# GpSimd keeps only the maxima across partitions in the first group; its clamps, memsets and low halves of weights go to VectorE and ScalarE

## The chip, the core and the metric

The kernel runs on one core of a Trainium2 chip. The core has five engines that run their own instruction queues and meet at semaphores: TensorE (PE, with its weight loads as PEld), VectorE (DVE), ScalarE (ACT), GpSimd (POOL) and SyncE (SP, which here issues every DMA). The metric is the device time of one execution in microseconds (us), lower is better; a comparison quotes the median of several executions.

## The reference: what is computed

Attention inside chunks of 64 positions, and then a two-layer network on its output:

```python
scores = scale * np.matmul(q_c, k_c.transpose(0, 1, 2, 4, 3))   # 8 batches, 8 heads, 9 chunks of 64x64
attn = np.exp(scores - max); attn = attn / (sum + 1e-09)
x = (attn @ v_c) put as (4608 tokens, 512)
h = x @ w_in            # 512 -> 2048
g = h - np.tanh(h)
out = g @ w_out         # 2048 -> 512
```

All of it is in float32.

## The kernel before, in words

**Tiling.** Tokens are taken 128 at a time (a "pair" of chunks): 36 pairs, in nine groups of four (512 tokens). For each group the network runs over 16 columns of 128 in the hidden layer (fc = 0 to 15): `gemm1` makes `ph` from x and w_in, `shrink` makes g from `ph`, and `gemm2` adds g times w_out into the four output tiles `po`. To reach float32 accuracy each operand is cut into a high and a low half (x: `xh`, `xl`; w_in: `wih`, `wil`; g: `gh`, `gl`; w_out: `woh`, `wol`), and three matmuls are made instead of one.

**Scales.** The 16-bit halves need a power of two as scale. For two fc of w_in at a time (index j = 0 to 7), for the values v of four pairs, and in the later groups for q, k and v, ScalarE sums absolute values per partition (`spread`, tiles named `junk`, result in `sums`). `power` then clamps the sums from below with TINY (POOL, tile `wall` or `xall`), takes the maximum across partitions (POOL, `partition_all_reduce`, tile `wtop` or `xtop`), and on DVE keeps the exponent bits (`from_w`, `earlyfrom`) and inverts (`to_w`, `earlyto`). `wih` and `wil` wait for `to_w`; `xh` and `xl` wait for `earlyto`.

**The first group** also has everything that is done once: the 16 MB of weights arrive as 64-bit patterns (`raw_in`, `raw_out`), `merged` turns them into float32 with one ACT and three DVE instructions per fc, and `weights` cuts the halves. `wol` (w_out minus its high half) is made on DVE for fc 0 and 1 and on POOL for the other 14. The attention of the first eight pairs (class `Early`) runs between this work. It keeps q and v in block-diagonal tiles (`qbd`, `vbd`, four buffers each) whose empty corners are zeroed once; buffers 0 and 1 are zeroed on DVE and ACT, buffers 2 and 3 on POOL. `identity` for the PE transposes is also made on POOL.

**Order.** PLAN is a list of tokens. Up to its bar, SP and PE keep the order of the tokens as written, and a scheduler orders the other engines; behind the bar the scheduler orders all of them, with its own idea of how long things take. At run time each engine takes its own queue strictly in order. The tokens that the prediction uses: `S` scores of a pair, `T` its transpose (PE, line 161, tile `psa`<-`ident`,`s`), `V` its values (PE, line 261), `N`/`n` its softmax division (on DVE, or head by head on ACT, line 244), `F` filler matmuls, `c` the cutting of a weight, `g` gemm1 with `shrink`, `h` gemm2. PE does the last tokens before its first network matmul in this order: T1, V0, V1, F7, S3, T2, g0.0.

**The later groups** (1 to 8) run the network on finished weights; attention of the next group (class `Late`) runs beside it, with its q, k and v scales made by the same `power`.

Of the kernel before, what the change touches and what calls it, by code (L numbers as in the profile page):

```python
# [11 lines left out]
F32 = mybir.dt.float32  # L12
# [3 lines left out]
U32 = mybir.dt.uint32  # L16
AF = mybir.ActivationFunctionType
ALU = mybir.AluOpType
# [3 lines left out]
P = 128  # L22
# [17 lines left out]
TINY = 2.0 ** -100  # L40
EXPONENT = 0x7F800000
# [13 lines left out]
def attn_ffn_kernel(ctx: ExitStack, tc: tile.TileContext, qE, kE, vE, qL, kL, vL, w_in, w_out, out):  # L55
# [7 lines left out]
    nc = tc.nc  # L63
# [11 lines left out]
    wo = [[None, None] for _ in range(FC)]  # L75
# [16 lines left out]
    def spread(pool, a, out):  # L92

        shape = [a.shape[0], *a.shape[1:]]
        junk = pool.tile(shape, BF16, name=f"junk{math.prod(shape[1:])}", bufs=1)
        nc.scalar.activation(junk, a, AF.Abs, scale=2.0 ** -12, accum_out=out)

    def power(pool, name, sums, to, back):


        n = sums.shape[1]
        al = pool.tile([P, n], F32, name=f"{name}all", bufs=2)
        nc.gpsimd.tensor_scalar_max(al, sums, TINY)
        top = pool.tile([P, n], F32, name=f"{name}top", bufs=2)
        nc.gpsimd.partition_all_reduce(top, al, channels=P, reduce_op=bass_isa.ReduceOp.max)
        if back.shape[1] < n:
            nc.vector.reduce_max(out=back, in_=top, axis=AX.X)
            top = back
        nc.vector.tensor_single_scalar(back.bitcast(U32), top.bitcast(U32), EXPONENT, op=ALU.bitwise_and)
        nc.vector.reciprocal(out=to, in_=back)  # L110


# [12 lines left out]
    def merged(w, raw):  # L125
        low, up = raw[:, :, 0], raw[:, :, 1]
        nc.scalar.activation(w.bitcast(F32), up.bitcast(F32), AF.Abs, scale=2.0 ** -112)
        nc.vector.tensor_single_scalar(w, w, 3, op=ALU.logical_shift_left)  # L128
        nc.vector.scalar_tensor_tensor(out=w, in0=low, scalar=29, in1=w, op0=ALU.logical_shift_right, op1=ALU.bitwise_or)  # L129
        nc.vector.scalar_tensor_tensor(out=w, in0=up, scalar=0x80000000, in1=w, op0=ALU.bitwise_and, op1=ALU.bitwise_or)  # L130

    def weights(pool, fc, part):
        if part:
            w = pool.tile([P, DM], U32, name="w_out", bufs=2)
            merged(w, raw_out.pop(fc))
            w = w.bitcast(F32)
            nc.scalar.copy(out=wo[fc][0], in_=w)
            (nc.vector if fc < 2 else nc.gpsimd).tensor_sub(wo[fc][1], w, wo[fc][0])  # L138
            return
        j, i = divmod(fc, 2)  # L140
        if i == 0:
            w_in_f[j] = pool.tile([P, 2, DM], U32, name="w_in", bufs=2), pool.tile([P, 2], F32, name="wsum", bufs=2)
        w, sums = w_in_f[j]
        merged(w[:, i], raw_in[j][:, i])
        w = w.bitcast(F32)
        spread(pool, w[:, i], sums[:, i:i + 1])
        if i == 0:
            return
        to = to_w[:, j:j + 1]
        power(pool, "w", sums, to, from_w[:, j:j + 1])  # L150
        h, l = wi[j]
        for i in range(2):
            nc.scalar.activation(h[:, i], w[:, i], AF.Copy, scale=to)  # L153
            nc.vector.scalar_tensor_tensor(out=l[:, i], in0=w[:, i], scalar=to, in1=h[:, i], op0=ALU.mult, op1=ALU.subtract)  # L154
# [9 lines left out]
    class Early:  # L164
# [3 lines left out]
        def __init__(self, pool, psum, bufs, zeros):  # L168
            self.pool, self.psum, self.st, self.bufs = pool, psum, defaultdict(dict), bufs
            self.qbd, self.vbd = (  # L170
                [pool.tile([P, 4, P, 2], F32, name=f"{n}{i}", bufs=1) for i in range(bufs)] for n in ("qbd", "vbd")
            )
            for i in range(bufs):
                for t in self.qbd[i], self.vbd[i]:
                    for r, o in ((slice(0, D), slice(D, P)), (slice(D, P), slice(0, D))):
                        if i > 1:
                            nc.gpsimd.memset(t[r, :, o], 0.0)
                        elif t is self.qbd[i]:
                            nc.vector.memset(t[r, :, o], 0.0)
                        else:  # L180
                            nc.scalar.copy(out=t[r, :, o], in_=zeros[r].rearrange("p (hp d two) -> p hp d two", hp=4, two=2))
# [16 lines left out]
        def powers(self, ps_):  # L198

            sums = self.pool.tile([P, len(ps_)], F32, name=f"vsum{len(ps_)}", bufs=1)  # L200
            for j, p in enumerate(ps_):
                spread(self.pool, self.st[p]["v"].rearrange("p hp d two -> p (hp d two)"), sums[:, j:j + 1])
            to, back = (const.tile([P, 1], F32, name=f"early{n}{ps_[0]}") for n in ("to", "from"))
            power(self.pool, "x", sums, to, back)
            for p in ps_:
                self.st[p]["to"] = to
            return back
# [63 lines left out]
    class Late:  # L271
# [16 lines left out]
        def sums(self, g, n):  # L288

            d = self.st[f"g{g}"]  # L290
            if n == "q":
                d["sums"] = self.pool.tile([P, 3], F32, name="sums", bufs=2)
            some = self.raw[n][:, :SIZES[g]]
            spread(self.pool, some, d["sums"][:, "qkv".index(n):"qkv".index(n) + 1])
            if n != "v":
                return
            d["to"], d["from"] = (self.pool.tile([P, 3], F32, name=m, bufs=2) for m in ("to", "from"))
            power(self.pool, "x", d["sums"], d["to"], d["from"])
            d["exp"] = self.pool.tile([P, 1], F32, name="exp", bufs=2)
            nc.vector.scalar_tensor_tensor(out=d["exp"], in0=d["from"][:, 0:1], scalar=scale, in1=d["from"][:, 1:2], op0=ALU.mult, op1=ALU.mult)  # L300
            from_x[g] = d["from"][:, 2:3]
# [171 lines left out]
    pool = first.enter_context(tc.tile_pool(name="first", bufs=2))  # L473
# [2 lines left out]
    nc.vector.memset(warm, 0.0)  # L476
    ident = pool.tile([P, P], F32, name="ident", bufs=1)
    make_identity(nc, ident)
    att = Early(pool, [psum, ps_a], 4, warm)


# [3 lines left out]
    def step(token):  # L485
# [17 lines left out]
        elif kind in "ME":  # L503
            att.largest(n)
            att.exponents(n, summed=kind == "E")
        elif kind in "Nn":
            att.sums(n)
            att.normalise(n, by_head=kind == "n")
        elif kind == "T":
            att.transpose(n)  # L510
            att.weights(n)
        elif kind == "V":
            att.values(n)
            att.result(n, *((x, n) if n < SIZES[0] else (nx, n - SIZES[0])))
        elif kind == "c":
            for k in (0, 1) if part is None else (part,):
                weights(raw, n, k)
        elif kind == "g":
            ff.gemm1(n, *((0, 4) if part is None else (2 * part, 2 * part + 2)))
            ff.shrink()  # L520
        elif kind == "h":
            ff.gemm2()
        elif kind == "Y":
            first_psum.close()
            att.psum = [ps_a]
            ps_o2 = ctx.enter_context(tc.tile_pool(name="ps_o2", bufs=1, space=PSUM, reuse_waits="tile"))
            ff.room(ps_o2, range(2, 4))
            pools.append(ps_o2)
        elif kind == "Z":
            first.close()  # L530
            late = ctx.enter_context(tc.tile_pool(name="late_weights", bufs=1, reuse_waits="tile"))
            weight_tiles(late, range(EARLY_FC, FC))
# [62 lines left out]
```

## Time and profile before

| | us |
|---|---|
| median of 3 runs (lowest, highest) | 915.82 (914.55, 917.6) |
| the profiled execution's own time | 919.06 |
| its span, first to last instruction | 917.2 |
| PE busy | 871.7 (95%) |
| DVE busy | 533.2 (58%) |
| ACT busy | 469.5 (51%) |
| POOL busy | 43.6 (5%) |

The profiled execution took 1.86 us more than its span, and 3.24 us more than the median of the three runs. PE is busy 95% of the span as an average; the slices of the span show where the other 5% lies. Idle time of an engine is put down in the profile to the instruction that ended it, or to "issue", where the engine waited for nothing that the profile shows.

### The profile page before, as it was taken

How to read it: one execution, taken by the hardware profiler on the slowest of the kernel's cores; microseconds unless marked ns; L12 is line 12 of the kernel's file. 1: busy time of each engine (PE TensorE's matmuls, PEld its weight loads, DVE VectorE, ACT ScalarE, POOL GpSimd, SP SyncE). 2: the span in 40 equal slices, each digit the busy share in tenths (PEclk: the TensorE clock that was granted, in tenths of full speed). 3: DMA queues.
4: the chain of work that ended last, by engine and by line, in shares of the span. 5: the costliest groups of instructions: out<-in, count | busy, mean ns of one | idle time of the engine just before them, and what ended most of it. 6: DMA issues, size and time to landing. Idle time of an engine off the chain costs nothing.

```text
span 917.2 us, 13175 instructions
## 1 busy us (share of the span) xinstructions
PE 871.7 (95%) x5163; PEld 571.1 (62%) x5163; DVE 533.2 (58%) x940; ACT 469.5 (51%) x820; POOL 43.6 (5%) x70
## 2 busy tenths in 40 slices
PE   7379897799999999999999999999999999999997
PEld 5367763456665666566656665666566666665665
DVE  4758686539776557555755575557555755533222
ACT  6548765357664646464646464646464644333221
POOL 2002121320000000000000000000000000000000
PEclk7779899999999999999999999999999999999999
DMA  8682232034222212220222122212221011001001
GB/s 230 211 243 74 93 118 88 1 138 103 67 72 81 58 24 74 77 58 24 72 78 58 25 73 77 58 24 73 77 58 25 12 47 24 13 12 46 1 1 46
DMA packets 61373, 62.71 MB, mean 68 GB/s; under 512 B 32640, under 2 KB 40832, under 8 KB 61312
## 3 DMA queue, kind: packets, MB, share of 16 engines
q1 hardware_dynamic: 61312, 61.88, 23.4%
q8 instruction: 40, 0.66, 0.3%
q14 instruction: 21, 0.17, 0.1%
HBM read 45.09 MB, written 9.44 MB: 59 GB/s over the span
## 4 chain that ended last, share of the span: by engine, by line
PE 84%; DVE 5%; issue 5%; ACT 4%; POOL 1%; DMA 1%; SPq 0%; ACTq 0%; POOLq 0%; DVEq 0%
PE po L437 40%; PE ph L416 38%; PE psa L362 2%; PE psa L328 2%; PE psa L261 1%; PE psa L213 1%; ACT s L231 1%; DVE w_in L129 1%; POOL wol L138 1%; DVE w_in L130 1%; ACT wih L153 1%; DVE w_in L128 1%; DVE w_out L129 0%; DVE w_out L130 0%; DVE t L425 0%
## 5 line engine op out<-in xcount | busy, mean ns | idle before, releaser
L437 PE MATMUL po<-woh,gh 128*128 128x512 f32 x576 | 245.7, 428 | 2.8 <-ACT gh L428 2.8
L437 PE MATMUL po<-wol,gh 128*128 128x512 f32 x576 | 227.0, 395 | 2.3 <-POOL wol L138 2.3
L437 PE MATMUL po<-woh,gl 128*128 128x512 f32 x576 | 225.8, 395 | 1.3 <-DVE gl L429 1.3
L425 DVE SCALAR_TENSOR_TENSOR t<-ph,sig,t 128x512 f32<-128x512 f32 (+1 forms) x148 | 108.7, 734 | 168.2 <-ACT t L424 168.2
L416 PEld LDWEIGHTS <-wih 128*128 128x128 f16 x1184 | 106.8, 99 | 156.8 <-issue 41.5
L424 ACT ACTIVATE t<-ph,sig 128x512 f32<-128x512 f32 (+1 forms) x148 | 99.9, 675 | 165.4 <-PE ph L416 165.1
L416 PE MATMUL ph<-xh,wih 128*128 128x512 f16 (+1 forms) x592 | 150.3, 377 | 24.2 <-ACT xh L268 16.5
L429 DVE TENSOR_TENSOR gl<-t,gh 128x512 fp32r<-128x512 f32 (+1 forms) x148 | 101.5, 686 | 114.3 <-ACT gh L428 114.1
L428 ACT CAST gh<-t 128x512 fp32r<-128x512 f32 (+1 forms) x148 | 89.5, 604 | 133.5 <-PE po L437 93.2
L416 PE MATMUL ph<-xl,wih 128*128 128x512 f16 (+1 forms) x592 | 149.3, 375 | 0.0
L416 PE MATMUL ph<-xh,wil 128*128 128x512 f16 (+1 forms) x592 | 149.1, 374 | 0.0
L437 PEld LDWEIGHTS po<-woh,gh 128*128 128x128 f32 x576 | 109.0, 189 | 33.7 <-ACT gh L428 4.4
L437 PEld LDWEIGHTS po<-wol,gh 128*128 128x128 f32 x576 | 108.8, 189 | 25.0 <-POOL wol L138 3.6
L437 PEld LDWEIGHTS po<-woh,gl 128*128 128x128 f32 x576 | 108.1, 188 | 25.9 <-DVE gl L429 2.6
L416 PEld LDWEIGHTS <-wil 128*128 128x128 f16 x592 | 57.9, 98 | 66.8 <-DVE wil L154 1.3
L320 DVE SCALAR_TENSOR_TENSOR v16l<-rawv,to,v16h 64x512 f16<-64x512 f32 x56 | 41.7, 745 | 3.8 <-ACT v16h L319 2.9
L311 DVE SCALAR_TENSOR_TENSOR q16l<-rawq,to,q16h 64x512 f16<-64x512 f32 x56 | 41.6, 743 | 2.2 <-ACT q16h L310 1.4
L319 ACT ACTIVATE v16h<-rawv,to 64x512 f16<-64x512 f32 x56 | 40.1, 716 | 4.9 <-PE psa L362 3.4
L310 ACT ACTIVATE q16h<-rawq,to 64x512 f16<-64x512 f32 x56 | 40.2, 718 | 3.1 <-DVE exp L300 1.2
L336 ACT ACTIVATE s<-s,exp 128x512 f32<-128x512 f32 x28 | 20.1, 720 | 30.1 <-DVE s L335 30.1
L348 ACT CAST a<-s 128x512 f16<-128x512 f32 x28 | 17.2, 615 | 21.6 <-DVE s L342 19.5
L460 DVE COPY t<-po 128x512 f32<-128x512 f32 x18 | 12.4, 691 | 26.7 <-PE po L437 14.3
(98 smaller groups left out, 779.8 us busy)
## 6 DMA issues: line engine op xcount, KB each, us to landing
out<-t SPq DMA_DIRECT2D x36, 256.0 KB, 2.1
raw_in<-w_in SPq DMA_DIRECT2D x16, 512.0 KB, 5.3
raw_out<-w_out SPq DMA_DIRECT2D x16, 512.0 KB, 3.6
rawq<-qL SPq DMA_DIRECT2D x28, 256.0 KB, 2.7
rawk<-kL SPq DMA_DIRECT2D x28, 256.0 KB, 2.9
rawv<-vL SPq DMA_DIRECT2D x28, 256.0 KB, 2.6
qbd<-qE SPq DMA_DIRECT2D x16, 128.0 KB, 4.2
k<-kE SPq DMA_DIRECT2D x8, 256.0 KB, 4.5
```

What stands on the lines that cost most here:

```text
L310: nc.scalar.activation(qh[r, :, r], q[r], AF.Copy, scale=to[r, 0:1])
L311: nc.vector.scalar_tensor_tensor(out=ql[r, :, r], in0=q[r], scalar=to[r, 0:1], in1=qh[r, :, r], op0=ALU.mult, op1=ALU.subtract)
L319: nc.scalar.activation(vh[r, :, r], v[r], AF.Copy, scale=to[r, 2:3])
L320: nc.vector.scalar_tensor_tensor(out=vl[r, :, r], in0=v[r], scalar=to[r, 2:3], in1=vh[r, :, r], op0=ALU.mult, op1=ALU.subtract)
L328: nc.tensor.matmul(ps[:, h], lhsT=q[a][:, h], rhs=d["k"][:, b, h], start=(k == 0), stop=(k == 2))
L336: nc.scalar.activation(s, s, AF.Exp, scale=d["exp"])
L416: nc.tensor.matmul(ph, lhsT=wi[fc // 2][a][:, fc % 2, kc * P:(kc + 1) * P], rhs=x[b][:, kc, cols], start=(k == 0), stop=(k == 3 * KC - 1))
L424: nc.scalar.activation(t, ph, AF.Tanh, scale=sig)
L425: nc.vector.scalar_tensor_tensor(out=t, in0=ph, scalar=sig, in1=t, op0=ALU.mult, op1=ALU.subtract)
L428: nc.scalar.copy(out=gh, in_=t)
L429: nc.vector.tensor_sub(gl, t, gh)
L437: nc.tensor.matmul(self.po[t], lhsT=gg[a][:, ts], rhs=wo[fc][b], start=(fc == 0 and i == 0), stop=(fc == FC - 1 and i == 2))
```

## The change

In `power` the clamp leaves POOL: the maximum across partitions is taken of the sums as they are, and the clamp is applied on DVE to the result. The 14 `wol` that POOL made are made on DVE. The corners of the block-diagonal buffers 2 and 3 are zeroed on DVE (`qbd`) and ACT (`vbd`). A maximum across partitions over a tile of ones, `ready`, whose result nothing reads, is put behind the making of the identity.

```diff
@@ power
         n = sums.shape[1]
-        al = pool.tile([P, n], F32, name=f"{name}all", bufs=2)
-        nc.gpsimd.tensor_scalar_max(al, sums, TINY)
         top = pool.tile([P, n], F32, name=f"{name}top", bufs=2)
-        nc.gpsimd.partition_all_reduce(top, al, channels=P, reduce_op=bass_isa.ReduceOp.max)
+        nc.gpsimd.partition_all_reduce(top, sums, channels=P, reduce_op=bass_isa.ReduceOp.max)
         if back.shape[1] < n:
             nc.vector.reduce_max(out=back, in_=top, axis=AX.X)
             top = back
-        nc.vector.tensor_single_scalar(back.bitcast(U32), top.bitcast(U32), EXPONENT, op=ALU.bitwise_and)
+        nc.vector.tensor_single_scalar(back, top, TINY, op=ALU.max)
+        nc.vector.tensor_single_scalar(back.bitcast(U32), back.bitcast(U32), EXPONENT, op=ALU.bitwise_and)
         nc.vector.reciprocal(out=to, in_=back)
@@ weights
-            (nc.vector if fc < 2 else nc.gpsimd).tensor_sub(wo[fc][1], w, wo[fc][0])
+            nc.vector.tensor_sub(wo[fc][1], w, wo[fc][0])
@@ Early.__init__
-                        if i > 1:
-                            nc.gpsimd.memset(t[r, :, o], 0.0)
-                        elif t is self.qbd[i]:
+                        if t is self.qbd[i]:
                             nc.vector.memset(t[r, :, o], 0.0)
@@ behind make_identity(nc, ident)
+    ready = pool.tile([P, 2], F32, name="ready", bufs=1)
+    nc.vector.memset(ready, 1.0)
+    nc.gpsimd.partition_all_reduce(ready[:, 1:2], ready[:, 0:1], channels=P, reduce_op=bass_isa.ReduceOp.max)
```

What becomes of the engines' queues. POOL's queue before, from the last memset on; a row "ISA" with no tiles is an instruction that moves no data, and "ISA wtop<-wall" is the maximum across partitions:

```order
L177 MEMSET vbd_129 64x4x128 x2
L103 TENSOR_SCALAR wall<-wsum 128x2
L105 ISA
L105 ISA wtop<-wall 128x2
L103 ISA
L103 TENSOR_SCALAR xall<-vsum_172 128x4
L105 ISA
L105 ISA xtop<-xall 128x4
L103 ISA
L103 TENSOR_SCALAR wall<-wsum 128x2
L138 TENSOR_TENSOR wol_79<-w_out,woh_77 128x512
L105 ISA
```

POOL's queue of the change, from the identity to the zeroing of the later groups' tiles:

```order
masks.py:199 AFFINE_SELECT ident<-ident 128x128
L479 ISA
L479 ISA ready<-ready 128x1
L103 ISA wtop<-wsum 128x2
L103 ISA xtop<-vsum_175 128x4
L103 ISA wtop<-wsum 128x2 x3
L103 ISA xtop<-vsum_915 128x4
L103 ISA wtop<-wsum 128x2 x4
L279 MEMSET v16h_1622 128x1024
```

The bare ISA rows, of which one stood at every turn between a maximum and another kind of work, are gone but for the one ahead of `ready`, and nothing but maxima stands between it and the memsets of line 279.

ACT's queue before, around the sums of the first four pairs' values (`junk`, `vsum`), the softmax division of pair 1 (L244) and `wih` of j = 0:

```order
L253 COPY aT<-psa 128x512
L244 ACTIVATE s<-s,sm 128x64 x8
L96 ACTIVATE junk_177,vsum_172<-vbd_128 128x1024
L96 ACTIVATE junk_179,vsum_172<-vbd_129 128x1024
L227 ACTIVATE s<-s 128x512
L253 COPY aT<-psa 128x512
L127 ACTIVATE w_out<-raw_out 128x512 x2
L153 ACTIVATE wih_70<-w_in,to_w 128x512 x2
```

And the same work in the change (L244 is now L241, L153 is L152):

```order
L241 ACTIVATE s<-s,sm 128x64 x4
L152 ACTIVATE wih_70<-w_in,to_w 128x512 x2
L96 ACTIVATE junk_180,vsum_175<-vbd_131 128x1024
L241 ACTIVATE s<-s,sm 128x64 x2
L96 ACTIVATE junk_182,vsum_175<-vbd_132 128x1024
L224 ACTIVATE s<-s 128x512
L241 ACTIVATE s<-s,sm 128x64 x2
L126 ACTIVATE w_out<-raw_out 128x512
```

`wih` moved ahead of the last two value sums, and the division of pair 1 is spread out around them.

DVE's queue before, at the last scale of the weights (j = 7):

```order
L129 SCALAR_TENSOR_TENSOR w_out<-raw_out,w_out 128x512
L130 SCALAR_TENSOR_TENSOR w_out<-raw_out,w_out 128x512
L107 TENSOR_REDUCE from_w<-wtop 128x1
L109 TENSOR_SCALAR from_w<-from_w 128x1
L110 RECIPROCAL to_w<-from_w 128x1
```

And in the change:

```order
L105 TENSOR_REDUCE from_w<-wtop 128x1
L127 TENSOR_SCALAR w_out<-w_out 128x512
L107 TENSOR_SCALAR from_w<-from_w 128x1
L129 SCALAR_TENSOR_TENSOR w_out<-raw_out,w_out 128x512
L108 TENSOR_SCALAR from_w<-from_w 128x1
L128 SCALAR_TENSOR_TENSOR w_out<-raw_out,w_out 128x512
L109 RECIPROCAL to_w<-from_w 128x1
L137 TENSOR_TENSOR wol_1111<-w_out,woh_1109 128x512
```

The clamp (L107) and a `wol` (L137) have joined the queue, and merges of w_out now stand between the steps of the scale.

## The prediction

> **What bounds the kernel now.** I read PE's busy time by stretches first, cut where PE's work changes. The columns are the stretch, its length, and the busy time of PE, PEld, DVE, ACT and POOL with the number of instructions, then the granted TensorE clock, the DMA share and GB/s. The last row is for DVE, further down.
>
> ```profile
> 0.00:31.80 31.80, 26.77 (x135) 20.34 (x135) 14.83 (x35) 18.87 (x51) 5.39 (x16) 0.79 0.77 215
> 31.80:48.20 16.40, 0.00 (x0) 0.10 (x1) 14.97 (x33) 11.23 (x23) 0.64 (x2) 0.59 0.76 239
> 48.20:67.90 19.70, 17.07 (x110) 14.34 (x109) 9.11 (x22) 7.60 (x19) 1.88 (x3) 0.82 0.82 242
> 67.90:139.00 71.10, 65.39 (x360) 48.31 (x359) 54.86 (x115) 54.17 (x161) 14.26 (x17) 0.95 0.28 101
> 139.00:184.20 45.20, 34.05 (x144) 19.70 (x144) 27.49 (x46) 19.42 (x33) 13.18 (x14) 1.00 0.11 39
> 184.20:276.20 92.00, 92.00 (x578) 59.31 (x578) 62.18 (x108) 60.20 (x89) 5.01 (x9) 1.00 0.36 95
> 20.30:184.20 163.90, 127.96 (x685) 91.92 (x684) 111.73 (x226) 98.54 (x246) 30.33 (x37) 0.90 0.37 121
> ```
>
> From 184.2 us on, where the second group begins, PE is busy without a break: nothing that POOL does there can be worth time. Everything to be had lies in the first group, where PE is idle 5.0 + 16.4 + 2.6 + 5.7 + 11.2 = 40.9 us. The timeline of PE says what ended the longest of those gaps (in brackets, the idle time before the row).
>
> ```profile
> 22.91 1.06 PE L161 MATMUL psa<-ident,s 128*128 128x128 f32 x4
> 31.16 0.61 PE L161 MATMUL psa<-ident,s 128*128 128x128 f32 x4
> 48.23 1.01 PE L416 MATMUL ph<-xh,wih 128*128 128x256 f16 x4 [16.47 <-ACT xh L268]
> 95.32 0.66 PE L161 MATMUL psa<-ident,s 128*128 128x128 f32 x4 [2.33 <-ACT s L231]
> 155.99 1.04 PE L416 MATMUL ph<-xh,wih 128*128 128x512 f16 x4 [3.48 <-ACT wih L153]
> 172.53 1.04 PE L416 MATMUL ph<-xh,wih 128*128 128x512 f16 x4 [2.71 <-ACT wih L153]
> ```
>
> The first network matmul waits 16.47 us for the halves of x, the late ones for halves of w_in. Both kinds need a scale, so I followed the chain of work that ended last back into POOL.
>
> ```profile
> 19.25 0.25 POOL wall L103
> ...
> 19.86 9.63 issue
> 29.48 0.38 POOL wtop L105
> ...
> 37.29 7.88 issue
> 45.17 0.40 POOL xtop L105
> ```
>
> The clamp takes 0.25 us and the maximum 0.38 us, but ahead of the two maxima the chain has 9.63 and 7.88 us in which the profile shows no work. POOL's timeline, and the rows of line 105, tell what that is.
>
> ```profile
> 0.86 0.52 POOL L177 MEMSET qbd<- 64x512 f32 x1
> 9.21 0.28 POOL masks.py:199 TENSOR_SCALAR_AFFINE_SELECT ident<-ident 128x128 f32<-128x128 f32 x1 [7.83 <-issue]
> ...
> 98.80 0.37 POOL L105 PARTITION_ALL_REDUCE wtop<-wall  x1 [5.93 <-DVE w_in L130]
> 99.09 0.45 POOL L105 PARTITION_ALL_REDUCE xtop<-xall  x1
> ...
> L105 POOLq MODIFY_POOL_CONFIG  x32: 1/11/11, 19.8 to 704.3; - x32
> ```
>
> The queue has a MODIFY_POOL_CONFIG where POOL changes its kind of work, and behind it stand 5.9 to 10 us of silence; two maxima in a row (98.80, 99.09) have none between them; and a memset at 0.86 us runs ahead of the first silence, the one of 7.83. So the price belongs to the change of kind, and memsets need none of it. A scale costs one silence before its maximum and, since the next clamp or `wol` is of the other kind, a second one behind it.
>
> **The change part by part.**
>
> *Silences taken out.* With nothing but maxima in POOL's queue only the silence before `ready` stays. It begins behind the identity at 9.5 us and ends, by the shortest row (5.93) and the longest gap (9.63 and the 0.3 us ahead of it in the chain), between 15.4 and 19.5 us. The first sums of w_in are there at 19.25, so the first maximum ends at about 19.9 instead of 29.86, and ACT and DVE have halves of w_in 10 us earlier. The x scale is then no longer behind POOL but behind ACT:
>
> ```profile
> 19.44 2.02 ACT L244 ACTIVATE s<-s,sm 128x64 f32<-128x64 f32 x8
> ...
> 23.54 0.19 ACT L96 ACTIVATION_READ_ACCUMULATOR junk<-vbd 128x1 f32 x1
> 31.16 1.34 ACT L153 ACTIVATE wih<-w_in,to_w 128x512 f16<-128x512 f32 x2 [5.30 <-DVE to_w L110]
> ```
>
> The last value sum, ready at 23.73, slips by `wih` (1.34) to about 25; the x maximum ends at about 25.5 instead of 45.57. The division of pair 1 (19.44 to 21.46), now spread around `wih` and two value sums, ends where the last value sum did or a little behind, at 25 to 26, so T1 slips on PE from 22.91 to about 26.2. From T1 to the end of T2 (31.16 + 0.61) PE had 8.9 us of work in a fixed order, so the first network matmul stands at 35.1 instead of 48.23: **13 us**. Were the division not in the way it would be 16.4; if V0 and V1 also meet late halves of x, about 10.
>
> *48.2 to 67.9.* The 2.6 us of idle time there go if they came from a `wol` on POOL, which ran just ahead of them. In their place pair 3's softmax is late: it follows S3 on a DVE that between 31.8 and 48.2 is busy 91% of the time, and I put 2.5 us of new idle time for T3. The clock gives something back:
>
> ```profile
> 48.00:52.00 4.00, 3.77 (x19) 2.92 (x19) 2.79 (x5) 1.88 (x6) 0.00 (x0) 0.52 1.03 287
> 96.00:104.00 8.00, 8.00 (x33) 6.98 (x33) 5.96 (x17) 7.61 (x20) 0.74 (x2) 0.57 0.53 199
> ```
>
> After the long gap PE works for 4 us at a granted clock of 0.52, which is 1.9 us lost, and there is no long gap any more: **2 us**. The 8 us at 0.57, 3.4 us lost, I leave in the sum, since a gap of 2.33 us was enough to bring them. The Trainium skill, "TensorE: Matmul & The Clock Gate", section "Part 1: The HAM clock gate (the "warmup" mystery)", has the clock halve only after about 3.4 us without work. This trace does not agree in either direction: the clock fell after 2.33 us, and stayed at 1.00 from 139 us on in spite of the 3.48. By the rule, with no such gap left, those 3.4 us would be saved too and the sum would be 28 instead of 25.
>
> *67.9 to 184.2.* In the last 45.2 us, where a maximum comes every 16.5 us (the two `wih` waits at 155.99 and 172.53), PE is busy 75%; in the 71.1 us before, 92%. I let the last stretch reach 92%, that is 34.05 / 0.92 = 37.0, a gain of 8.2, and take 2 us of the 5.7 idle ones before it: **10 us**. With no idle time at all it would be 16.9; with DVE as the new limit, nothing.
>
> *What DVE takes over.* Rows for its prices, and for what POOL cost it:
>
> ```profile
> 33.56 0.69 DVE L138 TENSOR_TENSOR wol<-w_out,woh 128x512 fp32r<-128x512 f32 x1
> 171.37 0.15 DVE L109 TENSOR_SCALAR from_w<-from_w 128x1 uint32<-128x1 uint32 x1
> ...
> 144.49 2.96 POOL L138 TENSOR_TENSOR wol<-w_out,woh 128x512 fp32r<-128x512 f32 x2 [7.47 <-ACT junk L96]
> 144.51 1.81 DVE L130 SCALAR_TENSOR_TENSOR w_in<-raw_in,w_in 128x512 uint32<-128x512 uint32 x1
> 146.24 1.76 DVE L429 TENSOR_TENSOR gl<-t,gh 128x512 fp32r<-128x512 f32 x1
> ```
>
> 14 `wol` of 0.69 are 9.7 us; ten clamps of 0.15 in the first group are 1.5. But beside POOL's two `wol` at 144.49 DVE's two instructions took 1.81 and 1.76, where the same kind of size takes 0.69: 2.2 us lost for two. If each of the 14 cost DVE as much it would get back 15; I count half of that, 7.5. Net 3.7 us more work (between -4 and 11), on an engine that in 67.9 to 184.2 is busy 82.4 of 116.3 us, 71%. In 106 us that would be 81%, and the 91% quoted above shows that it can do more. So I cost it at nothing; the cover is DVE's slack, and where that is gone it costs its 4 to 11 us. The four memsets that DVE gets and the four copies of ACT take by the 0.52 us of POOL's row some 2 us on each, before 6 us, where both engines wait for the first scores. The later groups' seven clamps cost 1 us of DVE beside a PE that is always busy: nothing.
>
> *Sum.* 13 + 2 + 10 = 25 us. The profiled execution took 919.06, so it would take 894; it stands 3.24 above the median, and off the median of 915.82 the sum gives 891 us, which I forecast.
>
> **The rivals.**
>
> 1. *DVE takes POOL's place.* `wol` stands in a strict queue ahead of merges and scales, and an engine that must also answer ACT and PE may not reach 81%. Then the first two terms come and little or nothing of the third, less up to 7 us of the work taken over: gain 8 to 17, 899 to 908. For it: the 91% between 31.8 and 48.2, work that now meets PE's start. Against: 71% over the rest.
>
> 2. *Hardly any idle time is left.* The gaps behind the first one and the 8 slow us go as well: gain 28 to 38, 878 to 888. For it: PE was kept at 92% with the silences in place. Against: the gap at 95.32 was ended by a softmax on ACT, not by a scale.
>
> 3. *Early transfers bind.* Up to 67.9 us the DMA share is 0.76 to 0.82, 53 us of full work; if nearly all of it were needed before the second scale of w_in, at about 51 us, it would take back some 5 us: 896. Against: much of it is for later weights.
>
> 4. *The silences stay.* If POOL must change over at each maximum for a reason that the pair at 98.80 and 99.09 doesn't show, nothing moves but DVE's work: 912 to 920.
>
> 5. *Slower, by DVE alone.* From the first scale (20.3 us) on DVE was busy 111.7 of 163.9 us, 68%, and now has 3.7 us more to do. If its waits for ACT and PE hold it to the same 68%, the group ends at 20.3 + 115.4 / 0.68 = 190 instead of 184.2, and the kernel takes 922. At 70.4% it decides: above that the change gains. The forecast, with the group ending at 159.2, needs 83%. For it: only a part of DVE's waiting is shown to hang on POOL. Against: the idle times at 155.99 and 172.53 do hang on it through `wih`.
>
> **How the numbers follow.** The forecast (gain 19 to 28, 888 to 897, the third rival's 896 being inside) has 0.48; the first rival 0.20, and 0.02 more where the third adds to it; the second 0.20; the fourth 0.04; the fifth 0.06. A change of 0.3% (2.7 us) is about what a measurement can tell from none. Faster is 0.48 + 0.22 + 0.20, and 0.01 of the fourth: 0.91; the same 0.03; slower 0.06. The range leaves out the outer half of the first, the last two and a little of the second: 879 to 903. The likeliest case's own range is 888 to 897.
>
> **What would show it.** In the changed profile: POOL with a single silence of 6 to 10 us behind the identity, and each maximum within a microsecond of its sums; the first network matmul at about 35 us; T3 some 2 us late; the second group starting at about 159 us; DVE busy 83% from 20 us to there. It is wrong if silences still stand before maxima, if the second group starts later than 172, or if PE's new gaps are ended by DVE instructions of lines 127 to 137.

## The result, and the profile after

The change takes 894.16 us (median of 4 runs, 890.42 to 895.63) against 916.71 us before (4 runs, 914.55 to 920.06): a ratio of 0.9745, 95% interval 0.9701 to 0.9788, 22.6 us less. A second series of five runs gave 893.28 us against 917.08: 0.975, interval 0.9724 to 0.9776. The forecast was 891.0 us, range 879 to 903.

The profiled execution of the change is the quickest of its four, 890.42 us with a span of 888.3; that of before took 919.06. The 28.6 us between these two are not the 22.6 between the medians, so I use a second profile of the change as well, an execution of 895.19 us.

From the page of the change: busy time and instructions by engine, and PE's and POOL's rows of busy tenths over 40 slices.

```profile
span 888.3 us, 13109 instructions
PE 866.5 (98%) x5163; PEld 566.8 (64%) x5163; DVE 538.5 (61%) x976; ACT 471.3 (53%) x824; POOL 15.5 (2%) x32
PE   7999898999999999999999999999999999999997
POOL 0000003000000000000000000000000000000000
```

PE is busy 98% instead of 95%. POOL fell from 43.6 to 15.5 us, and most of what is left in the first group is a block of memsets in one slice (the 3).

POOL's timeline (start, duration, work, and in brackets the idle time before it with what ended it):

```profile
7.88 0.28 POOL masks.py:199 TENSOR_SCALAR_AFFINE_SELECT ident<-ident 128x128 f32<-128x128 f32 x1 [6.95 <-issue]
14.88 0.38 POOL L479 PARTITION_ALL_REDUCE ready<-ready  x1 [6.71 <-DVE w_in L128]
17.19 0.37 POOL L103 PARTITION_ALL_REDUCE wtop<-wsum  x1 [1.94 <-ACT junk L96]
22.34 0.38 POOL L103 PARTITION_ALL_REDUCE xtop<-vsum  x1 [4.78 <-ACT junk L96]
46.35 0.37 POOL L103 PARTITION_ALL_REDUCE wtop<-wsum  x1 [23.64 <-ACT junk L96]
```

One silence is left behind the identity: POOL does nothing for 6.7 us before `ready`. After that each maximum waits only for its sums (`junk`, line 96). The 9.63 and 7.88 us that stood ahead of the first two maxima are gone. The instruction that the 6.71 is put down to differs between profiles (`w_in` here, `sm` of a softmax in the second one, with 6.9 us), so it is a chance neighbour; whether the silence belongs to `ready` itself is tested below.

PE's timeline at the places that the forecast named:

```profile
23.47 5.32 PE L258 MATMUL psa<-aT,vbd 128*128 128x64 f32 x32
28.58 3.19 PE L501 MATMUL ph<-warm 128*128 128x512 bf16 x7
...
34.17 0.60 PE L413 MATMUL ph<-xh,wih 128*128 128x256 f16 x4
41.55 0.60 PE L160 MATMUL psa<-ident,s 128*128 128x128 f32 x4
50.04 0.61 PE L413 MATMUL ph<-xh,wih 128*128 128x256 f16 x4 [0.60 <-ACT wih L152]
141.55 2.31 PE L413 MATMUL ph<-xh,wih 128*128 128x512 f16 x5 [2.59 <-ACT wih L152]
154.25 1.04 PE L413 MATMUL ph<-xh,wih 128*128 128x512 f16 x4
```

The first network matmul starts at 34.17 instead of 48.23, the one that stood at 67.90 now at 50.04, and the second group at 154.25 instead of 184.24. From there to the end of the span it takes 734.05 us, before 732.96: nothing was won behind the first group, and 1.1 us lost. One long gap is left, the 2.59 us at 141.55.

Busy time by stretches (stretch, length, busy PE, PEld, DVE, ACT, POOL; granted clock, DMA share, GB/s):

```profile
20.30:155.30 135.00, 124.86 (x683) 89.04 (x682) 112.41 (x246) 96.37 (x244) 11.49 (x17) 0.96 0.49 157
34.17:50.04 15.87, 14.69 (x115) 12.66 (x112) 13.79 (x33) 11.86 (x25) 0.37 (x1) 1.00 0.33 102
50.04:155.30 105.26, 97.47 (x505) 66.45 (x506) 90.30 (x195) 77.49 (x204) 10.74 (x15) 0.98 0.48 152
```

The first window reaches 1.05 us into the second group. DVE is busy 112.41 of its 135.00 us, 83%; before, it was busy 111.73 of 163.90. How much work was added does not follow from these two windows, since at 20.3 us the change has more of DVE's work behind it; it is counted from the start further down.

### The profile page after: what moved, and what is told of

The parts are those of the page before. It is cut to its first block, busy times and chain, and to the rows that moved or that the text cites. A ratio compares the mean times of both kernels' runs of the same rounds, so it can differ in the third digit from the quotient of the medians.

```text
span 888.3 us, 13109 instructions
## 1 busy us (share of the span) xinstructions
PE 866.5 (98%) x5163; PEld 566.8 (64%) x5163; DVE 538.5 (61%) x976; ACT 471.3 (53%) x824; POOL 15.5 (2%) x32
## 3 DMA queue, kind: packets, MB, share of 16 engines
q1 hardware_dynamic: 61312, 61.88, 23.8%
## 4 chain that ended last, share of the span: by engine, by line
PE 91%; ACT 4%; issue 2%; DVE 2%; DMA 0%; POOL 0%; ACTq 0%; DVEq 0%; POOLq 0%
PE po L434 42%; PE ph L413 40%; PE psa L359 2%; PE psa L325 2%; PE psa L258 2%; PE psa L210 1%; ACT junk L96 1%; ACT s L228 1%; PE ph L501 1%; ACT wih L152 0%; ACT w_out L126 0%; ACT s L241 0%; DVE w_out L127 0%; PE psa L160 0%; ACT w_in L126 0%
```

## The experiments

My theory after the first profile: POOL's silences were the whole loss, and DVE could take the work. The rivals: one part of the change gave nearly everything, or the end of contention between POOL and DVE, not of silences, was the gain. Two more questions came from the profile: what the gap at 141.55 is, and why runs of one kernel start their first network matmul at such different times. The table has, for the profiled execution of each kernel, its time, the start of the first network matmul, and what is left behind that start, beside the median.

| kernel | median | profiled | first network matmul | behind it |
|---|---|---|---|---|
| before | 916.71 | 919.06 | 48.23 | 870.8 |
| the change | 894.16 | 890.42 | 34.17 | 856.3 |
| the change, second series | 893.28 | 895.19 | 39.76 | 855.4 |
| clamps back on POOL | 915.92 | 917.95 | 41.14 | 876.8 |
| `wol` back on POOL | 906.51 | 906.34 | 37.72 | 868.6 |
| without `ready` | 895.11 | 893.85 | 37.70 | 856.2 |
| corners back on POOL | 891.18 | 893.61 | 36.70 | 856.9 |
| division ahead | 890.71 | 889.11 | 34.57 | 854.5 |
| corners on DVE | 896.17 | 894.71 | 38.59 | 856.1 |
| later zeroing on DVE | 890.49 | 890.49 | 39.03 | 851.5 |
| one filler for seven | 892.45 | 892.48 | 37.23 | 855.3 |
| the last two together | 889.8 | 890.0 | 36.58 | 853.4 |
| corners on POOL, later zeroing on DVE | 887.29 | 884.11 | 32.60 | 851.5 |

### The clamps back on POOL

```diff
+        al = pool.tile([P, n], F32, name=f"{name}all", bufs=2)
+        nc.gpsimd.tensor_scalar_max(al, sums, TINY)
-        nc.gpsimd.partition_all_reduce(top, sums, channels=P, reduce_op=bass_isa.ReduceOp.max)
+        nc.gpsimd.partition_all_reduce(top, al, channels=P, reduce_op=bass_isa.ReduceOp.max)
-        nc.vector.tensor_single_scalar(back, top, TINY, op=ALU.max)
-        nc.vector.tensor_single_scalar(back.bitcast(U32), back.bitcast(U32), EXPONENT, op=ALU.bitwise_and)
+        nc.vector.tensor_single_scalar(back.bitcast(U32), top.bitcast(U32), EXPONENT, op=ALU.bitwise_and)
```

> Only the clamps go back to GpSimd; the low halves of w_out stay on VectorE and the early memsets where the change put them. Theory (the silence at each change of kind on GpSimd was the price): a silence of 6 to 10 us stands again before every maximum or pair of maxima of the first group, the first network matmul comes at 40 to 46 us instead of 34, and the kernel takes 905 to 918 us. Rival A (the gain came from taking the low halves off GpSimd, where they blocked VectorE): 892 to 898, since those stay on VectorE. Rival B (it came from the early loads no longer waiting for GpSimd's memsets): also 892 to 898.

Measured: 915.92 us (10 runs; before 917.64, 15 runs), ratio 0.9982, interval 0.9965 to 0.9999. Only the clamps, some 0.25 us each, went back, and all but 1.7 us of the gain went with them. POOL's timeline of this kernel:

```profile
27.93 0.25 POOL L103 TENSOR_SCALAR wall<-wsum 128x2 f32<-128x2 f32 x1 [12.11 <-issue]
28.26 0.65 POOL L103 TENSOR_SCALAR xall<-vsum 128x4 f32<-128x4 f32 x1
36.33 0.76 POOL L105 PARTITION_ALL_REDUCE wtop<-wall  x1 [7.42 <-issue]
37.01 0.45 POOL L105 PARTITION_ALL_REDUCE xtop<-xall  x1
53.72 0.59 POOL L105 PARTITION_ALL_REDUCE wtop<-wall  x1 [7.17 <-issue]
```

The silences are back, 5.9 to 7.7 us ahead of the maxima of the first group, once for a pair of them, with `wol` still on DVE. The first network matmul is 7 us better than before, since here the first two scales share one pair of silences, and that is lost again behind it (876.8 against 870.8 us). Not all of that loss is time in which POOL is silent. The memsets of the later groups, which follow POOL's last maximum, here meet the last `wil` (DVE, PE):

```profile
164.32 5.81 DVE L154 SCALAR_TENSOR_TENSOR wil<-w_in,to_w,wih 128x512 f16<-128x512 f32 x2
170.20 1.89 PE L414 MATMUL ph<-xh,wil 128*128 128x512 f16 x4 [4.83 <-DVE wil L154]
```

The two `wil` end after 5.81 us where they take 1.41 in the change, and PE waits 4.83 us, against 2.59 at the change's memsets. And behind a wait of 3.50 us for the second x scale, which came late by a silence, the granted clock was 0.73, 0.50 and 0.50 in the three 8 us from 104 to 128 us. The scheduler also ordered the other engines anew. So the silences and what follows from them are the likeliest cause of most of the loss, and the run does not split it into its parts.

### The 14 `wol` back on POOL

```diff
-            nc.vector.tensor_sub(wo[fc][1], w, wo[fc][0])
+            (nc.vector if fc < 2 else nc.gpsimd).tensor_sub(wo[fc][1], w, wo[fc][0])
```

> Only the 14 low halves of w_out go back to GpSimd; clamps stay on VectorE. The first three maxima have only maxima ahead of them, later ones each have low halves between. Theory: the first network matmul stays at 34 to 36 us (no silence there), silences return before and behind the later maxima, the second stretch (second scale to the second group) loses most of its 12 us, total 899 to 908. Rival A (VectorE blocked while GpSimd works on low halves, silences worth little): VectorE instructions of 1.5 to 1.8 us beside them and 7 us lost, but no maximum late: 897 to 902, with the second group's start moved by VectorE and not by scales. Rival B (early loads): no change, 892 to 896.

Measured: 906.51 us (4 runs), 0.988, interval 0.9859 to 0.9901: some 12 us of the gain are lost. POOL and PE in this kernel:

```profile
56.98 4.67 POOL L137 TENSOR_TENSOR wol<-w_out,woh 128x512 fp32r<-128x512 f32 x2 [6.69 <-DVE t L422]
67.68 0.38 POOL L103 PARTITION_ALL_REDUCE wtop<-wsum  x1 [6.03 <-ACT t L421]
...
90.17 1.04 PE L413 MATMUL ph<-xh,wih 128*128 128x512 f16 x4 [2.76 <-ACT wih L152]
158.62 1.20 PE L413 MATMUL ph<-xh,wih 128*128 128x512 f16 x4 [2.71 <-ACT wih L152]
```

One silence before the `wol`, one before the maximum behind it, and PE waits for `wih` again. This is the 899 to 908 that the theory gave. The 12 to 13 us lie behind the first network matmul (868.6 against 856.3 or 855.4). So moving the clamps and the corners without the `wol` gives the first term of the forecast and little more. Some of the loss is the rival's and not the silences': beside POOL's `wol` at 78.30 two merges on DVE took 1.76 and 1.67 us instead of 0.68. The run does not separate the two.

### Without `ready`

```diff
-    nc.gpsimd.partition_all_reduce(ready[:, 1:2], ready[:, 0:1], channels=P, reduce_op=bass_isa.ReduceOp.max)
```

> The maximum over the tile of ones is left out; the queue then has its change of kind straight behind the identity, and the first maximum of w_in waits for its sums. Theory 1 (the silence is the change of kind itself, and runs when the queue reaches it): over by 15 us, the first maximum still at 17.2 us, 892 to 896. Theory 2 (the silence is paid by the first maximum that is called after it): the first maximum at 23 to 25 us, the first network matmul 4 to 7 us later, 897 to 901.

Measured: 895.11 us (4 runs), 0.9752, interval 0.9731 to 0.9772: the change's time. The first maximum of w_in in this kernel:

```profile
19.47 0.38 POOL L103 PARTITION_ALL_REDUCE wtop<-wsum  x1 [11.09 <-ACT junk L96]
```

It starts when its sums are there, with no `ready` ahead of it; its 19.47 instead of 17.19 us comes from later sums. The silence belongs to the change of config in POOL's queue, which POOL reaches behind the identity, and not to the first maximum; it runs while POOL would be waiting anyway. `ready` is worth nothing that can be measured.

### The corners of buffers 2 and 3 back on POOL

```diff
-                        if t is self.qbd[i]:
+                        if i > 1:
+                            nc.gpsimd.memset(t[r, :, o], 0.0)
+                        elif t is self.qbd[i]:
```

> Only the eight corner memsets of buffers 2 and 3 go back to GpSimd, where seven now stand behind the maximum named ready. Theory: memsets need no silence of their own, so GpSimd still has two in all; but they start at about 15 us instead of before 6, SyncE's queue stands at the third pair's load until then, and the x scale and the first network matmul come 3 to 5 us later (37 to 39 us): 895 to 900. Rival (a memset counts as a change of kind): silences also before the first scale, first network matmul at 43 us or later, 902 or more. Rival (loads are early enough anyway): 892 to 896.

Measured: 891.18 us (5 runs), 0.9702, interval 0.968 to 0.9724. I was wrong: moving the corners did not help the change; by the medians it cost some 2 to 3 us, and the interval only just reaches that of the change's second series. The memsets run between `ready` and the first maximum with no silence (POOL):

```profile
16.75 0.61 POOL L481 PARTITION_ALL_REDUCE ready<-ready  x1 [7.03 <-DVE w_in L128]
17.42 0.52 POOL L176 MEMSET qbd<- 64x512 f32 x1
21.60 0.37 POOL L103 PARTITION_ALL_REDUCE wtop<-wsum  x1
```

Behind the first network matmul nothing differs (856.9 us), so what they cost, if the medians are right, lies ahead of it. ScalarE's timeline gives a cause to test: here the division of pair 1 stands in one piece, ahead of the last value sums and `wih`.

```profile
21.32 2.02 ACT L243 ACTIVATE s<-s,sm 128x64 f32<-128x64 f32 x8
```

The next two runs test whether that order is the cause.

### The division put ahead; the corners on DVE

The first edit changes only the list of tokens, of which a part is shown, the second only where four corners are zeroed.

```diff
- E0 c0.0 c1.0 N0 T0 S2 F4 M1 M2 n1 c0.1 T1
+ E0 M1 n1 c0.0 c1.0 N0 T0 S2 F4 M2 c0.1 T1
```

```diff
-                        if t is self.qbd[i]:
+                        if t is self.qbd[i] or i > 1:
```

> The change, with the tokens M1 n1 moved ahead of c0.0 in the list: nothing moves to another engine, and the scheduler now puts the whole division of pair 1 on ScalarE ahead of the sums of w_in and of the last value sums; the sums of w_in and the first wih come later. Theory 1: what the corners on POOL gave came from ScalarE's order, so this gives it too: 890 to 892 us, T1 about 1 to 2 us earlier against the first scores than in the change. Theory 2: it came from taking the zeroing off DVE and ScalarE: no gain here, 893 to 895 us, or a loss by the later wih.

> The change, with the corners of vbd buffers 2 and 3 zeroed on DVE instead of ScalarE. The scheduler then puts the division of pair 1 on ScalarE behind both value sums and wih. Theory 1 (order): T1 comes 1 to 2 us later than in the change, 894 to 898 us. Theory 2 (load of ScalarE at the start): ScalarE is rid of four copies before the first scores, 890 to 893 us.

Measured, on one chip with the same runs of before: 890.71 us (5 runs), 0.9704, interval 0.9681 to 0.9726, with the division ahead; 896.17 us (5 runs), 0.9775, interval 0.9753 to 0.9798, with the corners on DVE, where the division comes last. ScalarE's timelines, the second profile of the change, then the division ahead, then the corners on DVE:

```profile
20.92 1.05 ACT L241 ACTIVATE s<-s,sm 128x64 f32<-128x64 f32 x4
22.28 1.33 ACT L152 ACTIVATE wih<-w_in,to_w 128x512 f16<-128x512 f32 x2 [0.31 <-DVE to_w L109]
24.56 0.57 ACT L241 ACTIVATE s<-s,sm 128x64 f32<-128x64 f32 x2
26.59 0.57 ACT L241 ACTIVATE s<-s,sm 128x64 f32<-128x64 f32 x2
```

```profile
17.74 1.53 ACT L241 ACTIVATE s<-s,sm 128x64 f32<-128x64 f32 x6
...
22.91 1.33 ACT L152 ACTIVATE wih<-w_in,to_w 128x512 f16<-128x512 f32 x2
```

```profile
22.16 1.33 ACT L152 ACTIVATE wih<-w_in,to_w 128x512 f16<-128x512 f32 x2 [1.38 <-DVE to_w L109]
23.92 2.00 ACT L241 ACTIVATE s<-s,sm 128x64 f32<-128x64 f32 x8
```

The division ends at 27.2, 19.3 and 25.9 us. Runs differ in how soon they get under way, so this is better counted from the end of PE's first 32 scores, at 13.2, 10.8 and 10.0 us: 14.0, 8.5 and 15.9 us. The first profile of the change gives 13.8 by the same count, the corners on POOL 9.4. With the division ahead V1 then waits for pair 1's copy on ScalarE, so that not all of this reaches the first network matmul:

```profile
25.83 3.68 PE L258 MATMUL psa<-aT,vbd 128*128 128x64 f32 x16 [4.34 <-ACT aT L250]
```

An edit that moves no work between engines gains what the corners on POOL gained, and one that takes copies off ScalarE but puts the division last loses instead. Both medians lie in the ranges of the theory of order, neither in those of its rivals. The loss with the corners on DVE need not be the order's alone: there the transpose of pair 0 also waits 4.23 us for a softmax on DVE, and `wih` starts 12.2 us behind the first 32 scores, in the change 8.9 and 9.1. The division ahead is the cleaner test. The 5.5 us between the division ahead and the corners on DVE lie outside both intervals; each apart from the change is 2 to 3 us and at the edge of what the runs can tell.

### The later groups' zeroing on DVE

```diff
-                nc.gpsimd.memset(t, 0.0)
+                nc.vector.memset(t, 0.0)
```

> The eight memsets of the later groups' tiles go from GpSimd to VectorE, behind the last halves of weights in its queue; all else as in the change. Theory (GpSimd's memsets block VectorE: the merge instruction of 0.42 us that took 2.84 us beside three of them, and PE's gap of 2.59 us): that instruction is back at 0.4 us, the gap at 141.55 shrinks to 0.3 us or less, 2 to 2.5 us faster than the change in the same call. Rival (that instruction was long for another reason): no difference within 1 us.

Measured: 890.49 us (5 runs), 0.9709, interval 0.9685 to 0.9733, on one chip with the second series of the change. First the change around its gap at 141.55 (POOL, DVE), then this kernel at the same place (DVE, PE):

```profile
136.27 1.02 POOL L279 MEMSET v16h<- 128x1024 f16 x1
...
138.05 1.02 POOL L279 MEMSET v16h<- 128x1024 f16 x1
136.51 2.84 DVE L127 TENSOR_SCALAR w_out<-w_out 128x512 uint32<-128x512 uint32 x1
139.27 0.13 DVE L107 TENSOR_SCALAR from_w<-from_w 128x1 f32<-128x1 f32 x1
```

```profile
141.37 0.42 DVE L127 TENSOR_SCALAR w_out<-w_out 128x512 uint32<-128x512 uint32 x1
144.00 1.25 PE L413 MATMUL ph<-xh,wih 128*128 128x512 f16 x5 [0.17 <-ACT wih L152]
```

In the change three memsets follow the last maximum on POOL (136.27 to 139.07), and a merge of w_out that started beside the first took 2.84 us and ended behind the third. The last scale of w_in stood behind it in DVE's queue, and PE waited 2.59 us for its `wih`. Without the memsets on POOL the merge takes 0.42 and PE's wait is 0.17. The median fell by 2.8 us, and each of the five runs is below each of the change's five beside them; the stretch behind the first network matmul fell by 4 between the two profiles.

### One filler instead of seven, and both edits

```diff
- V1 F7 S3
+ V1 F1 S3
```

> One filler matmul instead of seven stands before the scores of pair 3, everything else as in the change. Theory (with the x scale early, those fillers lie on PE's path to the first network matmul): it comes 1.3 to 2.8 us earlier and the kernel is 1 to 2.5 us faster than the change in the same call. Rival (PE waits there for the halves of x anyway, or its clock falls without the fillers): no difference or up to 2 us slower.

> The memsets of the later groups on VectorE and the short filler together. If both theories hold, the two gains add: 3 to 5 us faster than the change in the same call, 888 to 892 us. If the filler is worth nothing, 2 to 2.5.

Measured: 892.45 us (5 runs), 0.9733, interval 0.9709 to 0.9758, and with the zeroing on DVE too 889.8 us (5 runs), 0.9707, interval 0.9685 to 0.973. That is 0.8 and 0.7 us less than without the filler edit, within what runs differ by. PE in the second profile of the change and in the kernel with one filler:

```profile
27.48 6.93 PE L258 MATMUL psa<-aT,vbd 128*128 128x64 f32 x32
34.20 3.19 PE L501 MATMUL ph<-warm 128*128 128x512 bf16 x7
37.19 2.28 PE L210 MATMUL psa<-k,qbd 128*128 128x64 f32 x16
```

```profile
32.64 0.63 PE L501 MATMUL ph<-warm 128*128 128x512 bf16 x1
33.07 3.51 PE L210 MATMUL psa<-k,qbd 128*128 128x64 f32 x16
```

Of the 2.56 us of fillers taken out, the scores of pair 3 behind them took 1.23 back: 3.51 instead of 2.28.

### A version that beats both

The corners of buffers 2 and 3 on POOL and the later zeroing on DVE, edits shown above.

> Two earlier edits at once: the corners of buffers 2 and 3 zeroed on POOL again (that alone gave 891.2 us) and the later groups' zeroing on DVE (that alone gave 890.5). Theory 1: both gains are real and lie at different places (first transposes, last scale of w_in), so they add up: 886 to 889 us, the two-input merge beside the last scale at 0.42 us and the division of pair 1 whole and ahead of the last value sums. Theory 2: the gain of the first edit was a difference between batches of runs: 890 to 891 us.

Measured: 887.29 us (5 runs, 884.11 to 887.43; before 917.64, 9 runs), 0.9674, interval 0.9654 to 0.9694, which lies below both of the change's intervals. The two gains look as if they add: the median is 6.0 us below the change's second series, where one alone was 2.1 and the other 2.8. The intervals of the three kernels overlap, so the sum is not shown to the microsecond.

## Why the prediction was right, point by point

**The cause** was right: POOL's change of kind, and nothing that POOL computes. Two maxima in a row, and memsets, go without a silence; with the clamps back a silence stands before every maximum or pair of maxima of the first group again.

**First term, 13 us to the first network matmul.** The profiled pair shows 14.06, but the second profile 8.5, and without `ready` 10.5. That 14.06 is near 13 is luck: in that profile the last transpose of T1 starts at 23.30, 2.9 us before my 26.2, and from there to the end of T2 (34.34) it takes 11.0 us. With 14.5 to 15.4 us won behind that matmul (870.8 less 856.3 or 855.4) and 22.6 or 23.8 between the medians, its usual size is 7 to 9 us, as far as one profile of before can tell: I sized it 4 to 6 too large. Counted from the end of the first 32 scores (12.2 us before, 9.4 and 13.2 in the change) it is 11.3 and 9.5, 2 to 4 less than I said. Two steps of it failed. I gave T1 to the end of T2 the 8.9 us of before; in the second profile it takes 12.7 us from the last transpose of T1 (27.22) to the end of T2 (39.92), because V0, V1 and the fillers run at a lower clock: 6.93 + 3.19 us against 4.22 + 1.67. The spread division leaves holes on PE first:

```profile
24.00:28.00 4.00, 1.26 (x5) 0.97 (x6) 3.00 (x10) 4.00 (x11) 0.38 (x1) 0.52 0.34 136
28.00:32.00 4.00, 4.00 (x21) 4.00 (x21) 2.93 (x8) 1.58 (x3) 0.00 (x0) 0.50 0.10 16
```

PE is busy 1.26 of 4 us, and the clock is 0.52 and then 0.50. In the kernel that beats both, where the division is in one piece, V0 and V1 took 2.35 and 2.10 us, F7 1.67, and the first network matmul stood at 32.60. That the holes bring the low clock fits these profiles; no run tests it by itself. And T1 slipped to 27.22, 1 us behind my 26.2. Between the change's two profiles the first network matmul differs by 5.6 us (and by 0.8 the other way behind it). Of these 5.6, 3.7 are there when the first 32 scores end: in the second profile they start 0.9 later, behind the zeroing of `qbd` on DVE, and take 7.06 us instead of 4.23. Another 1.6 come from V0 and V1 (5.32 and 6.93 us).

**Second term, 2 us:** 3.8 in the profile (19.70 to 15.87). The clock is 1.00 there, as forecast, but the 2.5 us of idle time that I gave T3 did not come: it starts at 41.55 with no wait.

**Third term, 10 us:** 12.1 (116.3 to 104.2). PE's busy share from 50.04 to 155.30 is about the 92% that I took for the last part (97.47 of 105.26, 93%). Two things that I had not counted stood against each other: the collision with the memsets, which took some 3 us, and the 8 us at a clock of 0.57, which I had left in the sum and which did not come back (the clock is 1.00 from 40 to 140 us). The Trainium skill, "TensorE: Matmul & The Clock Gate", section "Part 1: The HAM clock gate (the "warmup" mystery)", would have taken those out, as no gap of 3.4 us was left. Here it was nearer than my step; but the first profile has the clock at 0.69 from 140 to 144 us, around the gap of 2.59, and the second has 1.00 around one of 2.60, so no length of gap decides it in these traces.

**DVE's extra work** was rightly costed at nothing. 83% busy was the forecast and 83% came, 2.4 us of it the merge that the memsets held. From the start to the second group DVE's busy time rose from 121.27 to 125.46 us, by 4.2, against the 3.7 of the sum and 2 for its memsets. `wol` took 0.685 us each as priced, and part came back as I had counted: the merges of w_in, 818 and 748 ns before, take 683 and 678 now, 3.3 us in all. The four memsets and the four copies were also put at nothing; that was wrong by 2 to 3 us if the runs on the corners are right, through the order of ScalarE's queue and not through the time of the copies.

**The rivals.** DVE as the new limit (899 to 908) did not come; keeping `wol` on POOL, the cure for it, gave 906.5. The silences stayed only where the clamps or the `wol` stayed on POOL. The case of hardly any idle time left came in part, as the clock's 8 us. Slower by DVE needed a busy share under 70.4%.

**The sum** of 25 us came out at 22.6 and 23.8: by the medians the first term too large by 4 to 6, the other two too small by 2 each, the rest behind the first group 1.1 the other way. The errors offset each other, so 891 against 894 is better than its steps were.

## What to carry to other kernels

Where a profile shows an engine that waits for nothing ahead of one kind of instruction, read its queue: on POOL a change between maxima across partitions and elementwise work cost 6 to 10 us each way here, memsets excepted, so such an engine gains by doing one kind of work even where another must do more. When a wait is removed, price what now stands in its place at the clock it will run at, and look at the order that a scheduler then gives the engine next in line. A memset on POOL that looks free can hold up VectorE; check what stands beside it.

## What the runs showed of the hardware

Memsets on POOL, which only write, held a one-input DVE instruction (TENSOR_SCALAR, 128x512) to 2.84 us where it takes 0.42 alone, and the time came back when they moved. The Trainium skill, "SBUF — State Buffer", section "Who interferes with whom", names `tensor_scalar` among the operations that can take the port pair shared with GpSimd, where one engine then blocks the other for a whole instruction; the trace agrees with the blocking, and shows it lasting over three memsets in a row, not one. With the clamps back on POOL, eight memsets in a row held a TENSOR_SCALAR over 128x8 for 6.56 us, which took 0.22 before. Neither my sum nor my rivals had that.

The first scores of the change (32 matmuls) took 7.06 us in the second profile at a clock that the profile gives as 1.00, while 16 of pair 3 took 2.28 later, and the same 32 took 4.23 in the first profile, also at 1.00. The seven fillers behind them took 3.19 us, as they do further on at a clock of 0.50, and 1.67 in the first profile. So the clock column may not tell the whole there; what slows them the runs don't show.
